# Three row blocks of w_k by the hardware DMA path in fp32, q loaded a batch ahead, and a new order of all work, in a fused linear-attention and channel-mix kernel

## The chip, the cores and the metric

The kernel runs on one core of one Trainium2 chip. The metric is the device time of one launch in microseconds (us). Executions of one kernel mostly agree within some tenths of a per cent here. A profile is one execution, and its span (first to last instruction) is about 1.8 us shorter than its time. Where a run is called slow, it lay more than 1.5% above the fastest of its kernel; ratios and comparisons use the other runs, called fast. Engines: PE is TensorE, DVE is VectorE, ACT is ScalarE, POOL is GpSimd, SP is SyncE.

## The reference

```python
# q, k, v: (8, 8, 576, 64) fp32 (batch, head, position, width); w_k: 512 x 1024, w_v: 1024 x 512, w_r: 512 x 512
kv  = einsum('bhsd,bhse->bhde', k, v)                  # linear attention, no softmax
o   = einsum('bhsd,bhde->bhse', q, kv)
x   = o / sqrt(mean(o*o, -1) + 1e-6) * g_norm          # RMS norm per head, then heads side by side: (8, 576, 512)
xp  = x moved down by one position
xk  = mu_k*x + (1-mu_k)*xp ;  xr = mu_r*x + (1-mu_r)*xp
out = sigmoid(xr @ w_r) * (relu(xk @ w_k)**2 @ w_v)
```

## The kernel before

Attention of eight batches (of 576 positions) runs ahead of the channel mix of nine groups (of 512 positions). The kernel holds a fixed order: each piece of work has a name, and a list of names says in which order the pieces are emitted. Each engine then executes its own pieces strictly in that order, so a piece that waits holds up all pieces behind it on its engine. `kv4.0` is the kv product of batch 4, `u4.00` a part of its q times kv, `k1.3`, `r1.0`, `v1.2.0` are parts of the three products of the mix in group 1, and `idle:N` is N filler matmuls of a zero tile. `ql4.1` copies q of two heads side by side (below a relay copy), `qt4.0` and `qt4.2` are the two DMA transposes of batch 4, and `gate4` is the gate behind them, shown in the code.

```python
# all q, k, v loads: fp32 in HBM, bf16 in SBUF, issued from GpSimd; two buffers for each of q, k, v
def load(b, n, h0, h1, due):
    nc.gpsimd.dma_start(out=kvq[n, b][:, h0:h1, :], in_=part(n, b, h0, h1))
...
# first heads of batch 0: three plain fp32 loads on the SP and ACT queues, then a cast
firsts = {n: first_load(n, eng) for n, eng in (("k", "SP"), ("v", "ACT"), ("q", "SP"))}
...
# w_k: two column halves, cast by the DMA
load_w(w_k_sb[:, :, cs], moe_w_k[:, cs], ...)
...
# from batch 3 on q is transposed by the DMA engines, not by PE:
#   ql: DVE or ACT copies q of two heads side by side (q2);  qt: the transpose, SBUF to SBUF
nc.sync.dma_start_transpose(out=qT[:, hs], in_=q2[:, hs])
...
# the gate: GpSimd reads an element of qT. Its later loads therefore go out only once qt has landed
gate = add({"POOL": 0.3}, lambda _: nc.gpsimd.tensor_copy(out=turned, in_=qT.t[0:1, 0, 0:1]), deps=[qtc[0]])
for n in ("k", "v", "q"):
    whole[(n, b + 1)].deps.append(gate)
```

## Time and profile before

| | kernel before |
|---|---|
| time, median of 3 runs | 203.49 us (203.48 to 204.22); the profiled run 203.43 |
| span of the profiled run, mean clock | 201.7 us, 0.997 |
| PE busy / DVE busy / ACT busy | 192.6 / 147.2 / 116.2 us |
| fillers on PE | 137, 12.3 us |

In the slices of the page each digit is a tenth of busy time in a fortieth of the span, about 5 us. In the timeline a line is: start, duration, engine, source line, operation, output and inputs, number of instructions, and in brackets the idle time just before it and what ended that.

### The profile page before, as it was taken

How to read it: one execution, taken by the hardware profiler on the slowest of the kernel's cores; microseconds unless marked ns; L12 is line 12 of the kernel's file. 1: busy time of each engine (PE TensorE's matmuls, PEld its weight loads, DVE VectorE, ACT ScalarE, POOL GpSimd, SP SyncE). 2: the span in 40 equal slices, each digit the busy share in tenths (PEclk: the TensorE clock that was granted, in tenths of full speed). 3: DMA queues.
4: the chain of work that ended last, by engine and by line, in shares of the span. 5: the costliest groups of instructions: out<-in, count | busy, mean ns of one | idle time of the engine just before them, and what ended most of it. 6: DMA issues, size and time to landing. Idle time of an engine off the chain costs nothing.

```text
span 201.7 us, 4116 instructions
## 1 busy us (share of the span) xinstructions
PE 192.6 (95%) x1629; PEld 103.4 (51%) x1651; DVE 147.2 (73%) x332; ACT 116.2 (58%) x148; POOL 33.4 (17%) x53
## 2 busy tenths in 40 slices
PE   7999899999999999999999989999999999999991
PEld 7867775454544454543457654444444444444451
DVE  1589988998898959799799985699486854432321
ACT  2588688666978597948723887268452226644020
POOL 7964314000050040040053010000200000000000
PEclk9999999999999999999999999999999999999998
DMA  6999999999969999999999949530742240003263
GB/s 173 200 202 207 204 205 205 204 203 248 171 100 200 217 217 193 173 207 216 207 251 248 203 70 231 156 104 5 185 143 51 66 132 15 2 0 101 69 193 108
DMA packets 39976, 31.69 MB, mean 157 GB/s; under 512 B 13812, under 2 KB 35092, under 8 KB 39956
## 3 DMA queue, kind: packets, MB, share of 16 engines
q0 software_dynamic: 21504, 18.11, 57.0%
q1 hardware_dynamic: 17780, 12.42, 25.9%
q10 hardware_dynamic: 672, 0.89, 1.3%
q8 instruction: 13, 0.21, 0.4%
q14 instruction: 7, 0.06, 0.1%
HBM read 35.33 MB, written 9.46 MB: 222 GB/s over the span
## 4 chain that ended last, share of the span: by engine, by line
PE 74%; DMA 13%; POOL 4%; ACT 3%; issue 2%; SPq 1%; DVE 0%; DVEq 0%; POOLq 0%; ACTq 0%
PE mm L795 25%; PE mm L875 24%; PE mm L853 12%; DMA w_k<-in_moe_w_k_dram 5%; DMA v<-in_v_dram 5%; DMA qT<-q 3%; PE at L649 2%; PE at L567 2%; PE mm L522 2%; PE mm L815 2%; PE mm L892 2%; PE at L892 2%; PE at L701 2%; POOL k L275 1%; POOL q L275 1%
## 5 line engine op out<-in xcount | busy, mean ns | idle before, releaser
L795 PE MATMUL mm<-xk,w_k 128*128 128x512 bf16 (+1 forms) x281 | 58.5, 355 | 0.4
L875 PE MATMUL mm<-w_v,sqk 128*128 128x512 bf16 x251 | 57.8, 379 | 0.6 <-issue 0.3
L799 ACT ACTIVATE relu<-mm 128x1024 bf16<-128x1024 f32 x36 | 36.9, 1024 | 27.1 <-PE mm L795 23.2
L795 PEld LDWEIGHTS <-w_k 128*128 128x128 bf16 x288 | 27.2, 98 | 26.7 <-issue 1.8
L875 PEld LDWEIGHTS <-sqk 128*128 128x128 bf16 x256 | 24.7, 98 | 29.2 <-issue 1.1
L853 PE MATMUL mm<-w_r,xr 128*128 128x512 bf16 x135 | 33.4, 379 | 0.8 <-issue 0.5
L879 DVE TENSOR_TENSOR out<-mm,sig 128x1024 f32<-128x1024 f32 x16 | 19.5, 1223 | 19.8 <-PE mm L875 15.8
L858 ACT ACTIVATE sig<-mm 128x1024 bf16<-128x1024 f32 x18 | 18.4, 1025 | 26.6 <-PE mm L853 26.5
L802 DVE TENSOR_TENSOR sqk<-relu 128x1024 bf16<-128x1024 bf16 x32 | 21.7, 687 | 10.9 <-ACT relu L799 10.7
L853 PEld LDWEIGHTS <-xr 128*128 128x128 bf16 x144 | 13.5, 98 | 15.6 <-issue 0.9
L185 ACT CAST uT<-at 128x576 bf16<-128x576 f32 x21 | 12.6, 641 | 12.2 <-PE at L649 12.2
L743 DVE TENSOR_SCALAR md<-d,cols 128x576 bf16<-128x576 bf16 x56 | 18.4, 371 | 0.3
L194 ACT ACT_TABLE_LOAD x12 | 15.4, 1283 | 0.2
L763 PE MATMUL mm<-zero 128*128 128x128 bf16 x137 | 12.3, 251 | 1.1 <-DVE zero L245 1.1
L717 DVE TENSOR_TENSOR xT<-uT,rs 128x1152 bf16<-128x1152 bf16 x14 | 10.5, 752 | 2.9 <-ACT rs L705 2.8
L656 DVE TENSOR_TENSOR sq<-uT 128x576 bf16<-128x576 bf16 x28 | 12.1, 451 | 0.8 <-ACT uT L185 0.6
L705 ACT ACTIVATE rs<-at,eps 128x576 bf16<-128x576 f32 x16 | 11.2, 738 | 1.8 <-PE at L701 1.7
L763 PEld LDWEIGHTS <-zero 128*128 128x128 bf16 x137 | 10.5, 116 | 2.9 <-issue 1.3
L684 POOL DMA_DIRECT2D rs<-rd x6 | 3.8, 634 | 44.2 <-DVE xk L746 20.6
L746 DVE TENSOR_TENSOR xk<-md,xT 128x1152 bf16<-128x1152 bf16 x14 | 10.6, 759 | 0.5
L746 DVE TENSOR_TENSOR xr<-md,xT 128x1152 bf16<-128x1152 bf16 x14 | 10.6, 759 | 0.5
L729 DVE TENSOR_TENSOR d<-xT 128x1152 bf16<-128x1152 bf16 x14 | 10.5, 753 | 0.2
(89 smaller groups left out, 175.2 us busy)
## 6 DMA issues: line engine op xcount, KB each, us to landing
out_dram<-out SPq DMA_DIRECT2D x22, 192.0 KB, 4.7
q<-in_q_dram POOLq DMA_DIRECT2D x6, 576.0 KB, 10.0
v<-in_v_dram POOLq DMA_DIRECT2D x6, 576.0 KB, 12.6
k<-in_k_dram POOLq DMA_DIRECT2D x6, 576.0 KB, 11.1
out_dram<-out SPq DMA_DIRECT2D x23, 128.0 KB, 2.2
rs<-rd POOLq DMA_DIRECT2D x6, 288.0 KB, 5.6
out_dram<-out SPq DMA_DIRECT2D x22, 64.0 KB, 6.6
w_k<-in_moe_w_k_dram POOLq DMA_DIRECT2D x2, 512.0 KB, 11.5
```

Of the source, the lines that this page charges most:

```text
L185: nc.scalar.copy(out=dst, in_=src)
L194: nc.scalar.preload_act_table_set(name)
L743: nc.vector.tensor_scalar(out=get(md)[:, hp], in0=d.t[:, hp], scalar1=cols[:, m0 + hp:m0 + hp + 1], scalar2=None, op0=ALU.mult)
L746: nc.vector.tensor_tensor(out=dst[:, hs, c0:c0 + S], in0=md.t[:, hs], in1=xT.t[:, hs, 0:S], op=ALU.add)
L763: nc.tensor.matmul(get(k_ps[i])[:, 0, 0:128], zero[:, 0:128], zero[:, 128:256], start=not k_seen[i], stop=not k_seen[i])
L795: nc.tensor.matmul(get(ps)[:, fc % 2, a0:a1], w_k_sb[:, cc, 128 * fc:128 * fc + 128], xk[:, cc, x0:x0 + a1 - a0], start=(cc == 0), stop=(c ...
L799: nc.scalar.activation(out=get(rt), in_=ps.t, func=AF.Relu)
L802: nc.vector.tensor_mul(out=get(sqk)[:, 2 * f2:2 * f2 + 2, :], in0=rt.t, in1=rt.t)
L853: nc.tensor.matmul(get(ps)[:, ci % 2, :], xr[:, cc, n0:n0 + 128], w_r_sb[:, cc, :], start=(cc == 0), stop=(cc == NHP - 1))
L858: nc.scalar.activation(out=get(sg), in_=ps.t, func=AF.Sigmoid)
L875: nc.tensor.matmul(get(ps)[:, ci % 2, :], sqk.t[:, fc, 128 * ci:128 * ci + 128], w_v_sb[:, fc, :], start=(fc == 0), stop=(fc == NFC - 1))
L879: nc.vector.tensor_mul(out=get(ot)[:, xs, :], in0=ps.t[:, xs, :], in1=sg.t[:, xs, :])
```

## The change

Its intent has two parts. First, w_k comes in row blocks, three of the four by the hardware path (issued from SP and ACT) as fp32 with a cast on DVE or ACT, so that the first products with w_k need not wait for all of it; all of batch 0 then goes by GpSimd. Second, from the gate of batch 3 on a gate releases k and v of the next batch and q of the one after it, so that only two loads that are needed soon follow each transpose. The whole order was planned anew for this.

```diff
-    firsts = {n: first_load(n, eng) for n, eng in (("k", "SP"), ("v", "ACT"), ("q", "SP"))}
+    (nc.sync if eng == "SP" else nc.scalar).dma_start(out=first_view(i), in_=moe_w_k[128 * i:128 * i + 128, :])
+    firsts = [first_load(i, eng) for i, eng in enumerate(("SP", "ACT", "SP"))]
...
-    l = load_w(w_k_sb[:, :, cs], moe_w_k[:, cs], -700 + 0.1 * i, 2.6, f"w_k{i}")
+    p_wk = [add({"DVE": ..., "ACT": ...}, lambda eng, i=i: copy(eng, w_k_sb[:, i, :], first_view(i)), ...) for i in range(3)]
+    p_wk.append(add({"POOL": 0.8}, lambda _: nc.gpsimd.dma_start(out=w_k_sb[:, 3, :], in_=moe_w_k[384:512, :]), ...))
...
-                for n in ("k", "v", "q"):
-                    whole[(n, b + 1)].deps.append(gate)
+                for n, at in (("k", b + 1), ("v", b + 1), ("q", b + 2)):
+                    if at < B:
+                        whole[(n, at)].deps.append(gate)
...
 the order (excerpts)
-... loadv3.0 loadk3.0 ... qt3.0 ... qt3.2 ... gate3 loadq4.0 ... loadk4.0 loadv4.0 kv4.0 ... gate4 loadq5.0 ... loadv5.0 loadk5.0 ...
+... loadk3.0 loadv3.0 ... qt3.2 ... qt3.0 ... loadq4.0 ... gate3 loadv4.0 loadk4.0 kv4.0 ... loadq5.0 ... gate4 ... loadk5.0 loadv5.0 ...
```

## The prediction

> **What bounds the kernel now.** I read the page first, parts 1 and 2: the busy shares and the forty slices (5 us each).
>
> ```profile
> PE 192.6 (95%) x1629; PEld 103.4 (51%) x1651; DVE 147.2 (73%) x332; ACT 116.2 (58%) x148; POOL 33.4 (17%) x53
> ...
> PE   7999899999999999999999989999999999999991
> ...
> PEclk9999999999999999999999999999999999999998
> DMA  6999999999969999999999949530742240003263
> ```
>
> TensorE is busy in every slice at a full clock, and the DMA engines are full for about the first 115 us and then idle much of the time. But part of TensorE's work is not useful: the group of line 763 (matmuls of a zero tile, the fillers that the order calls idle) is 137 instructions and 12.3 us. So next the table of waits, for TensorE alone, and its timeline up to 42 us and around 116 us:
>
> ```profile
> PE mm L763 <- DVE zero L245: 1.1, 1, 1.1
> PE mm L522 <- DMA w_k<-in_moe_w_k_dram: 0.6, 1, 0.6
> PE at L567 <- DMA v<-in_v_dram: 0.5, 1, 0.5
> ```
>
> ```profile
> 1.06 5.91 PE L763 MATMUL mm<-zero 128*128 128x128 bf16 x61 [1.06 <-DVE zero L245]
> ...
> 20.80 1.49 PE L522 MATMUL mm<-xk,w_k 128*128 128x256 bf16 x12 [0.59 <-DMA w_k<-in_moe_w_k_dram]
> ...
> 23.13 1.91 PE L522 MATMUL mm<-xk,w_k 128*128 128x256 bf16 x16
> ```
>
> The reader is to see two regimes. Up to about 23 us TensorE waits for data, mostly dressed up as fillers; from there to its last matmul at 197.5 us it is the bound, with one data wait of 0.5 us (the v of batch 7, at 116.46). Its whole idle time between 1.06 and 197.56 us is 196.5 - 192.6 = 3.9 us.
>
> Why does it wait early? The windows view of the first 23 us, cut where loads land:
>
> ```profile
> 10.00:12.50 2.50, 2.30 (x45) 1.59 (x41) 1.75 (x8) 2.26 (x6) 2.50 (x4) 1.00 1.31 200
> 12.50:17.30 4.80, 4.28 (x66) 3.05 (x61) 4.73 (x20) 4.25 (x13) 2.34 (x4) 1.00 1.30 204
> 17.30:22.70 5.40, 4.70 (x94) 3.91 (x94) 5.37 (x21) 3.43 (x8) 1.54 (x2) 1.00 1.24 207
> ```
>
> (Columns: stretch, length, busy PE, PEld, DVE, ACT, POOL, clock, DMA share, GB/s.) The last column stands at 200 to 207 whatever is loaded. Nearly all of these are casting loads, which write half of what they read, so this is about 400 GB/s read. The landings say the same: issue plus time to landing gives 6.6 us for the first two-head load and 12.5 for the ninth, so 8 loads of 2 x 576 x 64 x 4 = 295 KB in 5.9 us, 400 GB/s; the two column halves of w_k (1.05 MB each in fp32) land at 20.7 and 22.7, after v of batch 1 at 17.3: 2.10 MB in 5.4 us, 388 GB/s. So **the start is bound by fp32 bytes read, the rest by TensorE**. DVE is nearly as full there (4.73 of 4.80 and 5.37 of 5.40 us).
>
> **What the Trainium skill says.** "DMA: Bandwidth & Descriptors", section "Issuing engines are not separate DMA queues": loads issued from any engine share the same 16 engines, and another issuer only saves issue time. The trace agrees: read bandwidth is flat at about 400 GB/s, and GpSimd's issue (0.63 to 0.79 us per load) is not what the landings follow. The same page, "SWDGE vs HWDGE vs iDMA": a cast during a DMA can only be issued from GpSimd; so w_k through the other path comes as fp32 and needs a cast on DVE or ScalarE (the kernel before does that for its three first loads: 0.56 us on DVE, 0.83 on ScalarE for 96x768). "TensorE: Matmul & The Clock Gate", "Part 1: The HAM clock gate": about 107 ns per 128-column matmul cold, 56 warm. The fillers agree: about 104 ns apart up to 6 us, then about 56; so fillers added to the first group cost 0.056 us each.
>
> **The change, part by part.**
> 1. Bytes. Before the last part of w_k is in, both orders read the same: batch 0 (3.54 MB), half of batch 1 (1.77), w_k (2.10), 7.41 MB. Before, it landed at 22.7. After, the same bytes with the same start (first landings need about 2 us after the issue at 0.73) end at about **22.7** again: row block 3 of w_k replaces the second column half as the last. No gain in bandwidth.
> 2. What sits in front changes. Before, 0.88 MB went by the hardware path, and they were batch 0's own first heads. After, 1.57 MB of w_k (three blocks of 524 KB) go first, beside batch 0. Hence batch 0 is later: its first k (third load of the software queue) needs at most 1.57 + 0.885 = 2.45 MB to be read; at 400 GB/s from 2.2 us and some 1.7 us of latency that is about 10.0, where the first kv product ran at 7.43 before. The last load of batch 0 (1.57 + 3.54 = 5.11 MB) lands at 12.5 + 1.57 / 0.4 = 16.4, up to 17.1 by the first sum, where it was 12.5. So attention of batch 0 starts 2.5 us later and its last head pair has its data 4 us later.
> 3. What is gained: six of the eight first k parts (each 4 matmuls of 128x256, 0.44 us: 32 took 3.49) no longer need the last load. The new order puts four ahead of that load: 1.75 us of real work moved before 22.7. But it also moves two u products and one sum of squares (0.37 + 0.25 us) behind it.
> 4. Fillers: I added them in both orders: 137 before, 139 after; 76 of these at the start in place of 61 (15 x 0.056 = 0.85 us), fewer later. Real TensorE work is the same, instruction by instruction.
> 5. I added TensorE's pieces in both orders with the durations of the timeline. The first k part that needs all of w_k comes 16.5 us of pieces into the new order; the first k part of the old one came at 14.7 and really ran at 20.80. With the same offset less its wait (5.5), TensorE reaches it at 22.0; the load lands at 22.7; so it waits some 0.7 us, plus what early waits of part 2 push it. Say 22.8. From there to the first v product there are 11.2 us of pieces: 34.0, against 33.66 before: **+0.3**.
> 6. DVE: I added its pieces too. From the kv copy of the last head pair (17.4) to the last square that the first v product needs: 23.5 - 7.0 = 16.5 us, so 33.9. It ends level with TensorE, with no slack. Casts of w_k: 2 on DVE for 2 before, some 0.06 us more each; 1 on ScalarE. Small.
> 7. q ahead: the gate after the transpose of batch 6 now sits earlier, and only k and v of batch 7 are then needed, in 2/3 of the bytes. The wait at 116.46 goes: **-0.5**. The kv of batch 6 comes about 7 us earlier in the order, the others of batches 4 and 5 by 2 to 4 us. This buys slack for loads and transposes, not time: TensorE was not waiting there.
> 8. From the first v product on, TensorE's pieces are the same sum, and the mode switches between kinds of matmul number 72 for 69. The tail (last product, last store) is unchanged.
> Sum: 203.49 + 0.3 - 0.5 = 203.3. I lean a little lower, 203.1, because some of the 3.9 us of idle are small waits for other engines that the new order may avoid.
>
> **Rivals.**
> A. The hoped-for one: w_k early removes the early fillers' cause, and TensorE gains the 1.75 us moved ahead. For it: only a quarter of w_k is last. Against it: the fillers stay in the program, 139 of them, so TensorE's sum does not shrink. At the very best all data and engine waits vanish (3.9 us of idle, of which about 2 are small issue gaps): 201.6.
> B. DVE becomes the bound of the start. It was full from 10 to 23 us; data for batch 0 now come 2.5 to 4 us later, the same work has to follow, and an idle DVE at 8 to 14 us is lost. For it: parts 2 and 6. If it loses 2 us more than I count, the first group of outputs is late and TensorE, without fillers there, stands still: 205.5.
> C. The transfer is hidden anyway: q ahead changes nothing that TensorE sees, and the start comes out level: 203.0 to 203.5.
>
> **Range and chances.** The centre is C with a small net gain: 203.1. Down, the waits that can vanish set a floor: low 201.8. Up, B with half of its loss plus a late early load: high 205.2. Faster by over 2% needs under 199.4, below the floor of A: 0.02. Slower by over 2% needs over 207.6, twice B: 0.04. Within 2%: 0.94.
>
> **What would show it.** Part 1: the last block of w_k landing near 22.7, and 200 to 207 GB/s once only casting loads run. Part 2: the first kv product near 10, with TensorE waits of half a us or more before it on k, v or q of batch 0. Part 5: the last k parts of batch 0 after a wait for w_k, the first v product near 34.0. Part 6: DVE idle before 14 us, and none between 17 and 34. Part 7: no wait on v of batch 7. Fillers: 139, about 12.3 us. I am wrong if the hardware path reads faster than 400 GB/s or batch 0 isn't delayed by w_k (then A), if the late batch 0 stalls TensorE by more than 2 us (B), or if a reordered wait in the middle, which I haven't followed engine by engine, takes more than 1 us.

## More of the kernel before

One more view of the kernel before matters for what follows and isn't in the prediction: GpSimd's timeline, the four gates (the copies into `turned`) with the bracket saying how long GpSimd had stood there.

```profile
55.90 0.38 POOL L612 COPY turned<-qT 1x1 bf16<-1x1 bf16 x1 [22.17 <-DMA qT<-q]
71.96 0.18 POOL L612 COPY turned<-qT 1x1 bf16<-1x1 bf16 x1 [13.12 <-DMA qT<-q]
87.39 0.18 POOL L612 COPY turned<-qT 1x1 bf16<-1x1 bf16 x1 [12.60 <-DMA qT<-q]
104.16 0.60 POOL L612 COPY turned<-qT 1x1 bf16<-1x1 bf16 x1 [1.07 <-DMA qT<-q]
```

The reader is to see a chain: a gate opens, three loads go out, the q among them is copied and transposed, the transpose opens the next gate. A turn takes 15.4 to 16.8 us.

## The result and the profile after

The changed kernel takes 211.78 us (median of 4; 209.76 to 212.18) beside 203.49 (4 runs; 203.43 to 204.22): the ratio is 1.038, 95% interval 1.031 to 1.045. A ratio here is the mean time of one kernel's fast runs over that of the other's of the same rounds, so not quite the ratio of the medians. The change makes the kernel slower, where I had forecast no difference. The profiled run is the fastest of the four (span 208.0 us); the others had spans of 209.9 to 210.4.

The first page of the changed kernel, parts 1 and 2:

```profile
PE 194.6 (94%) x1632; PEld 103.7 (50%) x1653; DVE 147.0 (71%) x327; ACT 117.0 (56%) x153; POOL 33.6 (16%) x55
...
PE   7889999999969699999989999999999999999992
...
PEclk9999999999999969999999999999999999999998
```

PE is busy 2.0 us longer for the same work, one slice runs at a lower clock (0.6), and there are gaps in slices 12, 14 and 21, where the kernel before had none. The two largest waits of PE, and the lines of PE's timeline on which the reading rests (the first v product, u of batch 3, kv of batches 4 and 7):

```profile
PE at L647 <- DMA qT<-q: 2.5, 2, 1.7
PE at L564 <- DMA k<-in_k_dram: 1.9, 1, 1.9
```

```profile
34.08 3.62 PE L871 MATMUL mm<-w_v,sqk 128*128 128x512 bf16 x16
...
59.53 0.44 PE L647 MATMUL at<-qT,kv 64*64 64x288 bf16 x8 [1.66 <-DMA qT<-q]
...
72.66 0.95 PE L564 MATMUL at<-v,k 96*64 96x64 bf16 x48 [1.88 <-DMA k<-in_k_dram]
...
122.65 0.95 PE L564 MATMUL at<-v,k 96*64 96x64 bf16 x48 [0.28 <-DMA v<-in_v_dram]
```

The same three pieces (first v product, kv of batches 4 and 7) in the kernel before:

```profile
33.66 1.03 PE L875 MATMUL mm<-w_v,sqk 128*128 128x512 bf16 x4
...
73.58 0.95 PE L567 MATMUL at<-v,k 96*64 96x64 bf16 x48
...
116.46 0.95 PE L567 MATMUL at<-v,k 96*64 96x64 bf16 x48 [0.53 <-DMA v<-in_v_dram]
```

Two marks place the loss. The first v product starts at 34.08 (33.66 before): the start costs 0.4 us, where 0.3 was forecast. The kv product of batch 7 starts at 122.65 (116.46 before): 6.2 us, nearly the whole loss of this profile (208.0 - 201.7 = 6.3). From that product to the end both need the same, 85.35 and 85.2 us. So **nearly everything is lost between 34 and 123 us**, in the part of the kernel that I had called bound by TensorE.

GpSimd's timeline there, to be held against the gates shown above:

```profile
41.98 0.77 POOL L276 DMA_DIRECT2D q<-in_q_dram  x1 [9.87 <-PE at L625]
60.55 0.18 POOL L609 COPY turned<-qT 1x1 bf16<-1x1 bf16 x1 [17.80 <-DMA qT<-q]
61.09 0.77 POOL L276 DMA_DIRECT2D v<-in_v_dram  x1 [0.36 <-issue]
61.85 0.77 POOL L276 DMA_DIRECT2D k<-in_k_dram  x1
62.61 0.77 POOL L276 DMA_DIRECT2D q<-in_q_dram  x1
76.74 0.18 POOL L609 COPY turned<-qT 1x1 bf16<-1x1 bf16 x1 [13.35 <-DMA qT<-q]
...
91.44 0.18 POOL L609 COPY turned<-qT 1x1 bf16<-1x1 bf16 x1 [11.68 <-DMA qT<-q]
...
107.13 0.18 POOL L609 COPY turned<-qT 1x1 bf16<-1x1 bf16 x1 [12.84 <-DMA qT<-q]
```

The ungated load of q of batch 4 goes out at 41.98, and the first gate opens 4.65 us later than before. The later ones are 4.8, 4.05 and 3.0 us late. Each gate opens 0.4 to 1.5 us after the last load issued before it has landed: q of batch 4 landed at 59.1, of batch 5 at 76.3, of batch 6 at 90.7, of batch 7 at 106.6 (issue plus time to landing). This suggested a theory, called Q in the expectations: the one load ahead of the transposes of batch 3 sets the whole chain back.

I overlooked a second cause of the late first gate. In the new order `qt3.0`, whose output that gate reads, is issued behind `qt3.2`. In the trace's packet records the first of the two ends at 58.4 and the second at 60.0, and the gate opens at 60.55. In two kernels below that have the same q load in front and `qt3.0` first (before_q4_early, before_q_ahead) it opens at 58.9. So about 1.6 of the 4.65 us come from the order of the two transposes.

The clock: the windows view of the changed kernel, in steps of 1 us (stretch, length, busy PE, PEld, DVE, ACT, POOL, clock, DMA share, GB/s):

```profile
71.00:72.00 1.00, 0.00 (x0) 0.00 (x0) 0.08 (x1) 1.00 (x3) 0.00 (x0) 1.00 1.27 202
...
74.00:75.00 1.00, 0.78 (x3) 0.35 (x3) 1.00 (x3) 0.03 (x1) 0.00 (x0) 0.50 1.27 191
75.00:76.00 1.00, 1.00 (x4) 0.46 (x3) 0.47 (x1) 0.10 (x1) 0.00 (x0) 0.50 1.28 218
```

After the wait for k of batch 4 PE ran at half clock for 3.4 us, so that wait costs PE up to 1.7 us more than its 1.9.

### The profile page after: what moved, and what is told of

Read it like the earlier page. It is cut to its first block, busy times and chain, and to the rows that moved or that the text cites. A ratio compares the mean times of both kernels' runs of the same rounds, so it can differ in the third digit from the quotient of the medians.

```text
span 208.0 us, 4130 instructions
## 1 busy us (share of the span) xinstructions
PE 194.6 (94%) x1632; PEld 103.7 (50%) x1653; DVE 147.0 (71%) x327; ACT 117.0 (56%) x153; POOL 33.6 (16%) x55
## 4 chain that ended last, share of the span: by engine, by line
PE 65%; DMA 15%; issue 10%; ACT 3%; DVE 2%; SPq 1%; POOL 1%; POOLq 0%
PE mm L871 22%; PE mm L793 18%; PE mm L849 11%; DMA v<-in_v_dram 6%; DMA k<-in_k_dram 5%; DMA rows<-in_g_norm_dram 2%; PE at L888 2%; PE at L564 2%; DMA rd<-rc 2%; PE mm L813 2%; PE mm L888 2%; PE at L647 1%; PE mm L519 1%; PE at L699 1%; PE at L625 1%
## 5 line engine op out<-in xcount | busy, mean ns | idle before, releaser
L871 PE MATMUL mm<-w_v,sqk 128*128 128x512 bf16 x248 | 59.3, 385 | 0.8 <-issue 0.5
L761 PE MATMUL mm<-zero 128*128 128x128 bf16 x139 | 12.2, 247 | 1.1 <-DVE zero L246 1.1
L276 POOL DMA_DIRECT2D q<-in_q_dram x12 | 9.0, 751 | 15.8 <-PE at L625 13.8
```

Source lines behind the costliest of these rows:

```text
L761: nc.tensor.matmul(get(k_ps[i])[:, 0, 0:128], zero[:, 0:128], zero[:, 128:256], start=not k_seen[i], stop=not k_seen[i])
L871: nc.tensor.matmul(get(ps)[:, ci % 2, :], sqk.t[:, fc, 128 * ci:128 * ci + 128], w_v_sb[:, fc, :], start=(fc == 0), stop=(fc == NFC - 1))
```

## The experiments

Each set of experiments had its own runs of the kernel before beside it (medians 203.7 to 204.1 us), and the ratios are taken to these. The changed kernel wasn't run again, so differences to its 211.78 us are between sets.

### 1 to 4: which part, and which load

**start_only**: the changed order, loads and casts up to the first load of batch 2, then the order and gates of the kernel before.

```diff
 # changed kernel
+                for n in ("k", "v", "q"):
+                    whole[(n, b + 1)].deps.append(gate)
 # order: changed list up to "loadq2.0", then the list of before without what is already out
```

> The first part of the change alone: the order and the w_k loads of the changed kernel up to the first load of batch 2, then the order and the gates of the kernel before. Theory Q (the whole loss comes from the load of q of batch 4, which is issued ahead of the transposes of batch 3 and makes the gate chain start 4.65 us later): the start costs at most the 0.4 us seen at the first v product (34.08 against 33.66), so 203.5 to 204.5 us, and no wait over 1 us after 45 us. Rival W (w_k in fp32 by the hardware path costs the time, in a backlog on DVE that shows later): 207 us or more.

Measured: 203.71 us beside 203.81, ratio 0.999 (0.995 to 1.004). The w_k part neither costs nor gains anything that these runs can show (0.5% either way); rival W is out.

**rest_only**: the reverse splice, the start of the kernel before and the changed order and gates after it.

> The other part alone: the start of the kernel before, then the order and the gates of the changed kernel from the first load of batch 2. Theory Q: 208 to 212 us, with a TensorE wait of 1 to 3 us for qT near 58, a wait for k or v of batch 4 near 70 and a half-clock stretch of 3.4 us after it. Rival W: 203 to 205 us.

Measured: 214.14 us in the three fast runs (211.62 to 214.31; a slow one took 215.75), ratio 1.046 (1.039 to 1.054). The loss is all in the second part. The half-clock stretch that I expected isn't in this profile (clock 0.999), though the waits are: five for qT, 5.0 us in all, and three for k, 3.6 us. So the half clock isn't the core of the loss. This splice is some 2 us slower than the changed kernel itself, more than the 208 to 212 expected; the two halves weren't planned for each other, but no run shows that this is the reason.

**after_q4_gated_first**: the changed kernel with q of batch 4 back behind its gate.

```diff
-... loadq4.0 ql4.1:DVE ql4.3:DVE sq3.01 ql4.0:DVE k2.6 k2.7 uc3.00:DVE ksq2.1 ql4.2:DVE ... gate3 loadv4.0 loadk4.0 ...
+... sq3.01 k2.6 k2.7 uc3.00:DVE ksq2.1 ... gate3 loadq4.0 loadv4.0 loadk4.0 ... ql4.1:DVE ql4.3:DVE ql4.0:DVE ql4.2:DVE v1.2.1 qt4.0
```

> The changed kernel with one load moved: q of batch 4 is issued behind the gate of batch 3 (first of the three loads there) and its four relay copies stand later, just ahead of its transpose. Theory Q: the first gate opens at 55 to 57 us instead of 60.5, the 1.66 us wait for qT goes, and the wait for k of batch 4 with its half clock goes or falls under 1 us: 203.5 to 206.5 us. Rival O (not the loads but the new order of TensorE and DVE work costs the time): 209 to 212 us as before the edit, waits elsewhere.

Measured: 212.92 us in the three fast runs (211.27 to 213.24; a slow one took 215.08), ratio 1.042 (1.036 to 1.048). Theory Q fails in this form. The first gate did open at 57.0 and the wait near 58 went, but four loads now followed that gate, and the second one opened at 77.9, later than in the changed kernel. PE's timeline of this run:

```profile
71.61 0.95 PE L564 MATMUL at<-v,k 96*64 96x64 bf16 x48 [2.47 <-DMA k<-in_k_dram]
...
77.87 0.69 PE L647 MATMUL at<-qT,kv 64*64 64x288 bf16 x8 [3.23 <-DMA qT<-q]
```

**before_q4_early**: the kernel before with only that load moved ahead of the gate.

```diff
-... loadv3.0 loadk3.0 ... gate3 loadq4.0 ql4.2:ACT ...
+... loadv3.0 loadk3.0 loadq4.0 ... gate3 ql4.2:ACT ...
```

> The kernel before with that one load moved the other way: q of batch 4 without its gate, straight behind the loads of batch 3; nothing else changes. Theory Q: the transposes of batch 3 land 3.5 to 5 us later (gate at 59.5 to 61 instead of 55.9), TensorE waits 1 to 2 us for qT near 58; the order of this kernel wants k and v of batch 4 only at 73.6, so no second wait: 204.5 to 206.5 us. Rival O: 203.5 us, within 0.5.

Measured: 205.03 us beside 203.81, ratio 1.004 (1.000 to 1.009), the first gate at 58.94 and a wait of 1.20 us for qT there. A second one of 1.06 us, for qT of batch 6 at 109.7, was not expected. So the sign is as expected and the shift somewhat smaller (3.0 us where 3.5 to 5 were expected): 1.18 MB in front of a transpose put it off by 3.0 us, which is 390 GB/s. Here the next gate was back at 72.2, as two loads instead of three followed the first. One load in front costs about 1 us, not 8.

### 5 to 8: the loads without the new order, and the waits one by one

**before_q_ahead**: the kernel before with all q loads from batch 4 on a batch ahead, gates as in the change, other work in its old order.

```diff
-                for n in ("k", "v", "q"):
-                    whole[(n, b + 1)].deps.append(gate)
+                for n, at in (("k", b + 1), ("v", b + 1), ("q", b + 2)):
+                    if at < B:
+                        whole[(n, at)].deps.append(gate)
 # order: loadq4.0 behind loadk3.0, loadq5.0 behind loadv4.0, loadq6.0 behind loadk5.0, loadq7.0 behind loadv6.0
```

> The kernel before with only its q loads from batch 4 on moved a batch ahead, as in the change (gates and issue order of the loads), the order of all other work kept. The last call showed that the first gate shifts by 3.0 us with q of batch 4 in front (58.9 for 55.9), and that taking that load away from the changed kernel does not help it. Revised theory S (two things together: every transpose lands only when the loads issued before it have drained, so q ahead makes no gate earlier, and the changed order of TensorE wants kv and u of batches 4 to 6 up to 7 us earlier): gates stay about 16 us apart, 3 us later than before, and this order waits 1 to 3 us in all: 204.5 to 207 us. Theory L (the loads alone, without the new order, cost what the changed kernel lost): 209 us or more.

Measured: 208.81 and 207.79 us in the fast runs, 214.68 and 218.22 in the slow ones, ratio of the fast runs 1.023 (1.016 to 1.030). Neither theory: more than S said, less than L. By these two runs the loads alone, in the old order, cost some 4 us, about half of what the whole change costs. The profile fell in a slow run, so I take from it only the gates, 58.9, 76.2, 91.0 and 108.3, which are those of the changed kernel within 1.7 us, and what made this one run slow: PE stood 8.2 us for the second transpose of batch 6.

```profile
117.32 0.69 PE L651 MATMUL at<-qT,kv 64*64 64x288 bf16 x8 [8.18 <-DMA qT<-q]
```

By the packet records that transpose dragged on from 107.4 to 113.2 beside another transfer (the broadcast of batch 5's norm factors, `rs<-rd`); k and v of batch 7 had not begun. Why it was released only at 117.3, and whether the other slow run has the same wait, isn't known.

**after_kv4_later**: the changed kernel with kv of batch 4 behind three v parts and its u products behind two r parts.

```diff
-... kv4.0 relu2.0 kvc4.0:ACT v1.2.0 ... v1.2.1 qt4.0 u4.00 u4.01 uc4.01:ACT ... v1.3.0 v1.3.1 qt4.2 u4.11 u4.10 ... r2.2 r2.3 sig2.1
+... relu2.0 v1.2.0 ... v1.2.1 qt4.0 ... v1.3.0 kv4.0 kvc4.0:ACT v1.3.1 qt4.2 ... r2.2 r2.3 sig2.1 u4.00 u4.01 uc4.01:ACT ... u4.11 u4.10 ...
```

> The changed kernel, loads and gates untouched; on TensorE the kv product of batch 4 stands behind three parts of the v product of group 1 (2.6 us), and its four u products with their copies behind two r products (1.7 us more). Theory S: the 1.9 us wait for k of batch 4 and the half-clock stretch behind it go, so 2 to 4 us less than the changed kernel (211.8 median, 209.8 to 212.2): 206.5 to 209.5. Theory L: the wait only moves, 210 to 212.5.

Measured: 212.21 us (212.10 to 212.44). The wait for k went, and a new one of 4.22 us came for a copy on ACT a few us later, at 82.5. In the edited order that copy stands on ACT behind a relay copy of q of batch 5, and the profile shows the relay copy waiting 3.26 us for a transpose (`DMA qT<-q`) just after the gate of batch 4 (77.9). The wait only moved.

**after_fill_kv4**: the changed kernel with fillers in place of that wait.

```diff
             def kv_mm(_, hps=hps, hp0=hp0, ps=ps):
+                for _ in range(32 if b == 4 else 0):
+                    nc.tensor.matmul(get(ps)[:, 1, 0:128], zero[:, 0:128], zero[:, 128:256], start=True, stop=True)
```

> The changed kernel with 32 filler matmuls (128 columns, zero tile, into the unused half of the same PSUM tile; results unchanged) just ahead of the kv product of batch 4, where TensorE waits 1.9 us. If the half clock after that wait (3.4 us in the trace) comes from the gap and costs half of its length, the clock stays full and the time falls by 1 to 1.8 us in the runs that have it: median 210 to 211. If the gap is not the cause, the half clock stays and the time is the same or longer by up to 0.5 us.

Measured: 212.54 us (212.01 to 213.01): no gain. The clock did stay full around 73 us, so the gap was the cause of the half clock there. But PE, faster now, came early to the next gate's transpose and waited 1.06 us for it, where the changed kernel had no wait; and a wait of 2.14 us for qT of batch 6 at 110.5 was followed by a half clock of 3.4 us.

```profile
76.98 0.44 PE L649 MATMUL at<-qT,kv 64*64 64x288 bf16 x8 [1.06 <-DMA qT<-q]
...
110.49 0.32 PE L649 MATMUL at<-qT,kv 64*64 64x288 bf16 x4 [2.14 <-DMA qT<-q]
```

**after_q4_half**: the changed kernel with half of the ungated load.

```diff
+            elif (n, b) == ("q", 4):
+                whole[(n, b)] = load(b, n, 0, H // 2, -600 + b)
+                load(b, n, H // 2, H, -600 + b)
 # order: loadq4.0 (heads 0 to 3) where it was, loadq4.4 behind loadk4.0, ql4.3 and ql4.2 ahead of v1.2.1
```

> The changed kernel with the load of q of batch 4 in two halves: four heads where the whole load stood, four behind the loads of k and v of batch 4. If a transpose lands when the loads issued before it have drained, half the bytes in front (590 KB at about 400 GB/s) bring the first gate 1.5 us earlier: 59.1 instead of 60.5, with the wait for qT near 58 down from 1.7 to about 0.3 us. If the transposes are late for another reason (their place on the SP queue, the order of the two), the gate stays within 0.5 us of 60.5. Total time: not the point, 209 to 213.

Measured: first gate at 59.30 (59.1 expected, 60.5 before the edit), no wait for qT near 58. Half the bytes in front, 1.25 us earlier, with the transposes in the same places: the bytes in front do set when a transpose lands. The time was 212.34 all the same; the waits for k of batch 4 and for qT behind it stayed at 1.9 and 1.5 us.

In the four edits of the changed kernel so far (after_q4_gated_first and the last three here), what I took away in one place had come back as a wait at a later gate. That is how a kernel behaves that runs in lockstep with a chain: it can't be faster than the chain, whatever it does between two links. The theory became V: after 45 us the changed kernel runs at the pace of the chain gate, loads, transpose, gate.

### 9 and 10: fewer bytes in the chain

**after_small_q** and **before_small_q**: a quarter of each q load from batch 4 on, all other work as it is. The result is wrong (relative error 0.86 in both).

```diff
-            nc.gpsimd.dma_start(out=get(kvq[(n, b)])[:, h0:h1, :], in_=part(n, b, h0, h1))
+            h2 = h0 + 2 if n == "q" and b >= 4 else h1
+            nc.gpsimd.dma_start(out=get(kvq[(n, b)])[:, h0:h2, :], in_=part(n, b, h0, h2))
...
-                    frm = qin.t[:, 2 * hp:2 * hp + 2, :].rearrange(...)
+                    frm = qin.t[:, (2 * hp if b < 4 else 0):(2 * hp + 2 if b < 4 else 2), :].rearrange(...)
```

> The changed kernel with a quarter of each q load from batch 4 on (heads 0 and 1, which the relay copies then read for all heads; result wrong on purpose; order, gates, transposes and copies as they are). Theory V (after 45 us the changed kernel runs in lockstep with the chain gate, loads, transposes, gate; a wait taken away in one place comes back at the next gate): with 0.88 MB less per batch each turn of the chain is about 2.2 us shorter, the first gate comes at 58 instead of 60.5, kv of batch 7 about 8 us earlier than 122.65, and the time falls to 203 to 206 us. Theory O (the new order of TensorE, DVE and ScalarE work costs the time by itself, whatever the loads do): 208 us or more.

> The same cut of the q loads in the kernel before (result wrong on purpose), as the control. Theory V and theory O both: TensorE waited there only 0.5 us for the chain, so the time falls by 0 to 1 us: 202.7 to 204. If it falls by more, the chain cost the kernel before more than its waits show.

Measured: 203.12 us for the changed kernel (202.82 to 203.27) and 202.62 for the kernel before (202.57 to 203.71), beside 204.06 of the kernel before uncut. The same cut is worth 8.7 us in the one (211.78 to 203.12) and 1.4 in the other. PE's waits in the changed kernel with the cut, the first four lines, which are the largest that other engines or DMAs cause (none is for qT):

```profile
PE mm L762 <- DVE zero L246: 1.1, 1, 1.1
PE a L369 <- DMA v<-in_v_dram: 0.7, 1, 0.7
PE at L889 <- DVE out L896: 0.5, 1, 0.5
PE at L565 <- DMA v<-in_v_dram: 0.3, 1, 0.3
```

This settles the main question, and theory O is out. The changed order of PE, DVE and ACT work is within some 0.5 us of the old one if its data come in time. What fails is the chain. As V expected, the first gate opened at 58.0, and each turn was 1.8 to 3.0 us shorter (2.2 expected); kv of batch 7 came 6.6 us earlier, where I had said 8. In the control the fall was a little over what I expected (0 to 1 us), so the q loads cost the kernel before about 1 us, where its waits showed 0.5.

| run (us in its profile) | gate 3 | gate 4 | gate 5 | gate 6 | kv of batch 7 | from there to the end |
|---|---|---|---|---|---|---|
| before | 55.9 | 72.0 | 87.4 | 104.2 | 116.5 | 85.2 |
| start_only | 54.5 | 70.3 | 86.8 | 104.0 | 116.3 | 85.2 |
| after | 60.5 | 76.7 | 91.4 | 107.1 | 122.7 | 85.3 |
| rest_only | 61.2 | 77.5 | 94.4 | 111.0 | 127.1 | 85.4 |
| after_q4_gated_first | 57.0 | 77.9 | 92.3 | 108.3 | 124.1 | 85.4 |
| after_q4_half | 59.3 | 77.7 | 92.4 | 108.5 | 125.5 | 85.3 |
| after_small_q | 58.0 | 71.3 | 83.0 | 96.9 | 116.0 | 85.4 |
| before_small_q | 55.8 | 71.2 | 84.2 | 102.5 | 115.7 | 85.1 |

### 11: a version that might beat both

**before_kv7_later**: the kernel before with kv of batch 7 behind one k part.

```diff
-... loadk7.0 loadv7.0 kv7.0 loadq7.0 ... qt7.0 store3.0 k4.7 relu4.3 ...
+... loadk7.0 loadv7.0 loadq7.0 ... qt7.0 store3.0 k4.7 kv7.0 relu4.3 ...
```

> The kernel before with one TensorE piece moved: the kv product of batch 7, which waits 0.5 us for v, stands behind the next k part (0.87 us) that it does not depend on. Every kernel run so far ended 85.1 to 85.5 us after its kv product of batch 7, so taking that wait away should give 0.3 to 0.6 us: 203.0 to 203.7 beside 203.5 to 204 of before. If the place is not on the path: no difference.

Measured: 204.10 us (6 runs, 202.61 to 204.66) beside 204.06, where 203.0 to 203.7 was hoped for: no difference (ratio 0.9995, 0.996 to 1.003). In its profile the wait for v is gone and one of 1.6 us for qT stands at 109.4. No run points to a version that clearly beats the kernel before.

### 12 and 13: loads beside transposes

In the trace's records of single DMA packets (their clock runs about 10 us ahead of the span's) I counted, per us, the 768-byte packets of the casting loads and the 256-byte packets of the transposes:

```text
                 us of the record      loads per us   transposes per us
loads alone      52 (before)           263            0
both             66 (after)            188            183
both             98 (after)            186            188
transposes alone 97 (before)           0              995
transposes alone 64, 65 (before)       2, 0           752, 497
```

Beside each other, one packet of the one goes with one of the other. A load then gets 186 x 1536 bytes = 286 GB/s read instead of 404 (263 x 1536), and a transpose of 1152 packets (11,522 for ten) gets between a fifth and two fifths of its own pace (186 beside 995, 752 and 497). In the kernel before q is loaded, copied and transposed within one turn, and the transposes run mostly after the loads. In the changed kernel the next q comes last in the turn, and by the same records the transposes run beside it: those of batch 4 from 70.6 to 77.1 us of the span, q of batch 5 from 71.2 to 75.8, and likewise in the next two turns. So a transpose lands, and the gate opens, just after the next q. Only in the last turn, where no q is left, do they run beside v (116.5 to 122.5, v of batch 7 from 116.2 to 122.2). The last turn is what the next two kernels test.

**after_v7_first**: the changed kernel with v of batch 7 issued straight behind k of batch 7, ahead of a transfer that stood between them (`rb5`, `rs<-rd` in the profile, which broadcasts batch 5's norm factors). **after_v7_first_qt_late**: besides, the transposes of batch 7 held back until its kv product is done.

```diff
-... gate6 loadk7.0 k4.2 ... rb5 ... rr6 loadv7.0 kv7.0 ...
+... gate6 loadk7.0 loadv7.0 k4.2 ... rb5 ... rr6 kv7.0 ...
 # second kernel, besides:
-... ql7.3:ACT ... ql7.1:ACT ... kvc7.0:ACT qt7.2 ...
+... kvc7.0:ACT ql7.3:ACT ql7.1:ACT qt7.2 ...
```

> The changed kernel with the load of v of batch 7 issued straight behind that of k, ahead of the broadcast of batch 5's factors that stood between them (1.6 us later issue in the trace). If the broadcast is what makes v of batch 7 land 15.5 us after its gate (12.2 in the kernel before), it lands 1.5 to 3 us nearer to the gate: 12.5 to 14 us. Time by theory V: at most 0 to 2 us less than the changed kernel, since TensorE waited at earlier gates: 209 to 212.

> The last kernel with two relay copies of q of batch 7 moved on ScalarE behind the copy of kv of batch 7, so that no transpose of batch 7 is in flight beside its k and v. If transposes and loads share the engines packet by packet (186 and 186 per us beside each other, 265 loads per us alone, counted in the trace), v lands some 2 us nearer to the gate than in after_v7_first: 10 to 11.5 us, and the transposes themselves land in 4 to 5 us instead of 6.5. If it is not the transposes, the same as after_v7_first within 0.5. Time 208 to 212, not the point.

Measured, landing of v after the gate (both from the time to landing of that one load): 17.0 us in after_v7_first (15.5 in the changed kernel), 12.0 in after_v7_first_qt_late. The transposes took 9.5 us from issue to landing in the first and 3.6 in the second. So it isn't the broadcast's place in front that delays v: moving it away made v no earlier. With the transposes out of the way v comes 5 us nearer to the gate; I had expected 2. Not all of this can be put down to the transposes. The gate of this run opened 2.5 us later (110.0 for 107.5), so on the clock of the span v landed 2.4 us earlier (122.0 for 124.4). And by the packet records the broadcast, now behind v, ran beside the last packets of v in after_v7_first (118 to 122 us), as it ran beside the transposes, but hardly in the second run. That transposes and loads slow each other is shown by the counts above; how much of the 5 us is theirs isn't.

Both kernels are far slower, 219.16 and 218.58 us. That was a miss, I had expected 208 to 212, and its cause shows in DVE's timeline of after_v7_first:

```profile
126.25 0.76 DVE L715 TENSOR_TENSOR xT<-uT,rs 128x1152 bf16<-128x1152 bf16 x1 [8.28 <-DMA rs<-rd]
```

The broadcast of batch 5's factors, now behind k and v in the same queue, lands 15.5 us after its issue instead of 8.8, and DVE and then PE stand still for it. It's the same rule once more: what stands in front of a transfer decides when it lands.

## Why the prediction was wrong, point by point

- **Bytes, late batch 0, filler counts, first v product (parts 1 to 5): right.** The last block of w_k landed at 22.2 (22.7 forecast), the last load of batch 0 at 16.6 (16.4), the first kv product ran at 9.64 ("near 10"), fillers were 139 and 12.2 us, the first v product started at 34.08 (34.0). The forecast wait of 0.7 us for w_k did not show: fillers ran up to the k part at 22.5. Two figures in these parts were off without consequence: the "first sum" gives 16.7 for the last load of batch 0, not 17.1, and the slow fillers stood 107 ns apart, not 104. The early waits were fewer than forecast: 1.04 us for a copy on ACT and 0.53 for the small g_norm load, instead of several for q, k and v.
- **DVE (part 6): right.** From 20 to 30 us DVE was busy 9.9 of 10 us, and the start cost 0.4 us in all. start_only shows that this first part of the change is neutral.
- **q ahead (part 7): the step that failed.** It said that the gate after the transpose of batch 6 "now sits earlier", that the wait at 116.46 "goes: -0.5", and that the rest "buys slack for loads and transposes, not time: TensorE was not waiting there". The gate sat 3.0 us later, the wait stayed (0.28 us, at 122.65), and the rest cost 5.8 us between the first v product and kv of batch 7. I had counted the bytes behind each gate (two loads instead of three) and not those in front of it. The q that no longer stands between gate and k stands before the gate: the transposes behind the gate run beside the next q and land after it, 1.18 MB or 3.0 us later (before_q4_early). So the bytes ahead of k and v of any batch are the same as before, and the gates are one load later. Meanwhile the new order asked for kv of batch 4 at 70.8, where the old one took it at 73.6. Along the chain the 6.2 us add up like this: the first gate is 4.65 us late (3.0 for q of batch 4, 1.6 for the order of the two transposes), 1.7 of that is won back by the last gate, and v of batch 7 lands 15.5 us after that gate instead of 12.2. Of these last 3.3 us, 1.6 lie before its issue (the broadcast of batch 5's factors now stands there) and 1.7 in its landing, beside the transposes. This sum is read from two profiles. Only the 3.0 us were tested alone, and issuing v ahead of the broadcast (after_v7_first) did not bring it nearer to the gate.
- **The sign that was named.** The prediction's last sign of being wrong was a reordered wait in the middle of more than 1 us, "which I haven't followed engine by engine". Two came, 1.66 us for qT of batch 3 and 1.88 for k of batch 4. It had given slower by over 2% a chance of 0.04.
- **The reading behind that step.** I read that the DMA engines were full up to 115 us, and then put the DMA bound at the first 23 us only. "TensorE was not waiting" showed that the old order fitted the chain, not that the chain had slack. The 0.5 us wait for v of batch 7 was a hint of it.
- **The rivals.** A (the gain) and C (level) didn't come; B (DVE as the bound) didn't either. None of them was a chain through the DMA engines with PE following it, so the upper end of the range, 205.2, covered only a bad start.
- **The half clock** wasn't forecast. It can add up to 1.7 us where a wait of about 2 us drops the clock. But in after_fill_kv4 the time that PE won at 73 us was partly given back as a wait at the next gate, and among the four runs of the changed kernel the two with the fullest clock (0.995 and 0.996) took 211.6 and 211.9 us, the profiled one (0.989) 209.8. In lockstep, PE's own speed isn't what counts.

What stays open: why three of the four runs of the changed kernel are 2 us slower than the profiled one, why before_q_ahead spreads from 207.8 to 218.2 us, and how the loss divides between the later loads and an order that asks for them earlier (the loads alone cost some 4 of 8 us, by two runs).

## What to carry to other kernels

When loads are gated by a transfer, draw the chain gate, loads, transfer, gate, and count for each link the bytes issued before it; a load moved "a batch ahead" has not left the queue, it stands in front of something else. Look also at which of several transfers a gate reads, and keep that one first. A static order without waits proves only that it fits the present arrival times, so before moving pieces earlier, look at where their data land. To tell a costly order from a late chain, cut the bytes of the chain in both kernels, with a wrong result if need be, and compare the two falls.

## What the Trainium skill lacked or had wrong

- "DMA: Bandwidth & Descriptors", "Queues, rings and completion order", says that an engine goes round between its queue rows packet by packet. The packet counts fit that (186 and 188 per us beside each other). What it lacks is what follows for transposes: a transpose of 295 KB is 1152 packets of 256 bytes; it landed in 3.6 us with no q, k or v load beside it and in 9.5 us beside loads and a broadcast, and a transpose fell from 995 packets per us alone to 188 beside a load.
- The same page, "Rules for kernel authors", says that a transpose next to ordinary DMAs needs nothing. That holds for the data (all these results were correct), not for the time: beside transposes a casting load fell from 263 to 186 packets per us.
- The same page has no rate for casting loads. Here they ran alone at 263 to 266 packets of 1536 bytes read per us, 404 to 409 GB/s, within 1.2% of the 408.7 GB/s that its section "iDMA fabric — 4 AXI ports for 8 engines, asymmetric across TPBs" has for a lone stream of plain loads from SP.
- "TensorE: Matmul & The Clock Gate", "Part 1: The HAM clock gate", gives about 3.4 us of idle for the clock to drop. Here waits of 1.9 us (changed kernel) and 2.1 us (after_fill_kv4) with short matmuls around them were enough, and the half clock then lasted 3.4 us; but not every such wait is: after one of 1.8 us in rest_only the clock stayed full.
